# Weight loads of a decode step regrouped: wq and w1 in two loads each, w2 in one, wo in six

## The chip, the cores and the metric

The kernel runs on one core of one Trainium2 chip. The metric is the device time of one execution in microseconds (us). Kernels are compared only within the same rounds. "Faster" and "slower" mean a difference of over 2%. The profiled execution's own clock is the span, about 1.4 us shorter than the time.

TensorE does the matmuls, VectorE, ScalarE and GpSimd the rest of the arithmetic; SyncE issues the large loads, and 16 DMA engines carry them. In these profiles TensorE is granted either its full clock or half of it; the two matmuls of a row of wo follow each other every 0.215 us at the one and every 0.43 us at the other. "Half clock" below means the latter.

## The reference, cut to what matters

One token (batch 1, sequence 1, width 1024) goes through a layer norm, and then through two branches whose results are added to it:

```
xn = layernorm(x)
q  = xn @ wq                       # 1024 x 4096: 32 heads of 128
k, v = last 4096 rows of 4 key/value heads, each shared by 8 heads
attention = softmax(q k^T / sqrt(128)) v @ wo        # wo: 4096 x 1024
mlp = gelu(layernorm(xn) @ w1 + b1) @ w2 + b2        # w1: 1024 x 3584, w2: 3584 x 1024
out = x + attention + mlp
```

Each weight is used once, on one token. In bf16 that is 8.4 MB of wq, 4.2 of k, 7.3 of w1, 4.2 of v, 7.3 of w2 and 8.4 of wo: 39.85 MB to fetch, for little arithmetic.

## The kernel before

All large loads are issued on SyncE's queue in the order wq, k (2 blocks), w1, k (2 blocks), v, w2, wo. A weight is viewed as so many "rows" a partition, and a load takes a few rows, the same for all 128 partitions. The lists at the head say how many rows each load takes:

```
WQ_CHUNKS = [1, 3, 4]
W1_CHUNKS = [2, 2, 2, 2]
W2_CHUNKS = [14, 14]
WO_CHUNKS = [15, 9, 5, 2, 1]
WO_IN_W1 = sum(WO_CHUNKS[:2])
```

Each load has its own semaphore. GpSimd turns the landings of wq and w1 into row counts (L260), on which TensorE's loops wait row by row:

```
for sems, chunks, rows in ((s_wq, WQ_CHUNKS, r_wq), (s_w1, W1_CHUNKS, r_w1)):
    for j, nr in enumerate(chunks):
        pool.wait_ge(sems[j], 16)
        pool.sem_inc(rows, nr)
# ... cut ...
with nc.Fori(0, KC, 1, engines=TENSOR) as k:            # the h stage: xn @ w1
    pe.wait_ge(r_w1, k + 1)
    # ... 8 matmuls a row (L387) ...
```

TensorE's order is: q (L335), h (L387), the scores against k (L403, each block first transposed by VectorE at L344), PV (L504), w2 (L537), wo (L548) and the last row of wo (L557). w2 goes where wq was, so it is issued when q is done; 24 rows of wo go where w1 was, when h is done, and 8 rows where k was, when the scores are done. At the end TensorE takes wo's loads as they land:

```
pe.wait_ge(DVE.sem, d_op)
r = 0
for j, nj in enumerate(WO_CHUNKS[:-1]):
    pe.wait_ge(s_wo[j], 16)
    for _ in range(nj):
        for n in range(2):
            pe.matmul(ACC[n], lhsT=OP[:, r:r + 1], rhs=wo_at(r, 1)[:, n * 512:(n + 1) * 512],
                      start=False, stop=False)
        r += 1
# ... cut: the last load's row is done the same way in a block of its own (L557),
#     then the sums are copied (L567, L569) and stored ...
```

## Time and profile before

| | before |
|---|---|
| time, first 3 runs | 98.78 us median (98.74 to 98.83) |
| span of the profiled run | 97.7 us, granted TensorE clock 0.878 |
| fetched | 39.86 MB, 408 GB/s over the span |
| large loads | 22, of which 17 ahead of wo |
| TensorE matmuls busy | 68.9 us |

How to read it: a transfer that has been issued early stands in a queue, so its time to landing is mostly the time of what is ahead of it: wo's 9 rows land 42.1 us after their issue, and are 5.5 us of the stream themselves. The landing is the moment that counts, and it is the issue's start plus the time to landing. The 16 DMA engines work from about 1 us to about 95 us (SyncE's first packet of data starts at 1.01, wo's last packet ends at 94.75, and 36 of the page's 40 slices have a busy share of 90% or more), so the rest of the kernel can only add to that. The lines are shown in the prediction.

### The profile page before, as it was taken

How to read it: one execution, taken by the hardware profiler on the slowest of the kernel's cores; microseconds unless marked ns; L12 is line 12 of the kernel's file. 1: busy time of each engine (PE TensorE's matmuls, PEld its weight loads, DVE VectorE, ACT ScalarE, POOL GpSimd, SP SyncE). 2: the span in 40 equal slices, each digit the busy share in tenths (PEclk: the TensorE clock that was granted, in tenths of full speed). 3: DMA queues.
4: the chain of work that ended last, by engine and by line, in shares of the span. 5: the costliest groups of instructions: out<-in, count | busy, mean ns of one | idle time of the engine just before them, and what ended most of it. 6: DMA issues, size and time to landing. Idle time of an engine off the chain costs nothing.

```text
span 97.7 us, 1056 instructions
## 1 busy us (share of the span) xinstructions
PE 68.9 (71%) x330; PEld 32.0 (33%) x330; DVE 36.6 (37%) x49; ACT 5.8 (6%) x11; POOL 7.1 (7%) x23
## 2 busy tenths in 40 slices
PE   0002299959992999878996364279994799891991
PEld 0002255525541556435542112033341333330330
DVE  3708530000008999600999534794005300000002
ACT  0500060000001000000000000400000000000002
POOL 6795000000000000000000000000000000000000
PEclk9999999999999669999999955555699759999579
DMA  5999999999999999999999999999999999899960
GB/s 171 449 455 465 397 429 429 429 392 426 443 452 393 399 452 423 440 402 429 429 429 423 423 486 423 481 411 399 493 423 389 428 428 516 355 423 419 399 267 8
DMA packets 3205, 39.88 MB, mean 408 GB/s; under 512 B 370, under 2 KB 388, under 8 KB 644
## 3 DMA queue, kind: packets, MB, share of 16 engines
q1 hardware_dynamic: 3170, 39.85, 96.1%
q8 instruction: 1, 0.02, 0.1%
q10 hardware_dynamic: 34, 0.01, 0.1%
HBM read 39.86 MB, written 0.00 MB: 408 GB/s over the span
## 4 chain that ended last, share of the span: by engine, by line
DMA 84%; PE 9%; SPq 4%; issue 1%; DVE 1%; POOLq 0%
DMA W<-in_A_wo_dram 43%; DMA W<-in_B_w_dram 41%; PE PS L548 5%; PE PS L387 3%; SPq L178 1%; SPq L168 1%; SPq L162 1%; DVE KV L567 1%; SPq L426 0%; PE PS L557 0%; POOLq L260 0%
## 5 line engine op out<-in xcount | busy, mean ns | idle before, releaser
L344 DVE STREAM_TRANSPOSE KV<-KV 128x4096 bf16<-128x4096 bf16 x4 | 17.5, 4424 | 5.7 <-DMA KV<-in_A_k_cache_dram 5.7
L335 PE MATMUL PS<-WA,PT 128*97 x64 | 15.8, 410 | 1.4 <-POOLq L260 1.2
L387 PE MATMUL PS<-W,YZ 128*97 x64 | 14.7, 387 | 1.2 <-POOLq L260 1.2
L335 PEld LDWEIGHTS PS<-WA,PT 128*97 x64 | 8.6, 134 | 8.2 <-issue 4.1
L387 PEld LDWEIGHTS PS<-W,YZ 128*97 x64 | 8.6, 135 | 7.3 <-issue 4.6
L504 PE MATMUL PS<-KV,PT 128*32 128x512 bf16 x32 | 9.9, 484 | 0.1
L403 PE MATMUL PS<-KV,LQ 128*128 x32 | 7.8, 399 | 2.3 <-DVE KV L344 2.3
L548 PE MATMUL PS<-W,OP 128*1 128x512 bf16 x48 | 7.0, 451 | 2.2 <-DMA W<-in_A_wo_dram 2.2
L537 PE MATMUL PS<-WA,GT 128*1 128x512 bf16 x56 | 7.9, 452 | 0.0
L567 DVE CAST KV<-PS 1x512 bf16<-1x512 f32 x1 | 0.7, 683 | 18.8 <-PE PS L557 18.8
L347 DVE STREAM_TRANSPOSE TT<-PS 128x1024 f32<-128x1024 f32 x1 | 1.3, 1251 | 15.8 <-PE PS L335 15.8
L295 PE MATMUL PS<-XT,meanf 128*128 128x16 f32 x2 | 0.6, 386 | 9.1 <-DVE XT L291 9.1
L504 PEld LDWEIGHTS PS<-KV,PT 128*32 128x32 bf16 x32 | 3.7, 117 | 5.9 <-issue 4.0
L403 PEld LDWEIGHTS PS<-KV,LQ 128*128 x32 | 3.2, 99 | 6.5 <-issue 3.8
L548 PEld LDWEIGHTS PS<-W,OP 128*1 128x1 bf16 x48 | 2.2, 92 | 6.6 <-DMA W<-in_A_wo_dram 2.5
L537 PEld LDWEIGHTS PS<-WA,GT 128*1 128x1 bf16 x56 | 2.7, 96 | 4.7 <-issue 2.5
L295 PEld LDWEIGHTS PS<-XT,meanf 128*128 128x128 f32 x2 | 0.5, 312 | 9.1 <-DVE XT L291 9.1
L509 DVE TENSOR_TENSOR TT<-PS,RM 32x512 f32<-32x512 f32 x1 | 0.7, 679 | 7.1 <-PE PS L504 7.1
L451 ACT ACTIVATE Pe<-PS,NMB 128x512 bf16<-128x512 f32 x2 | 1.3, 684 | 29.0 <-DVE NMB L448 29.0
L205 DVE MEMSET PS<- 128x3072 f32 x1 | 2.6, 2618 | 0.6 <-issue 0.6
L569 ACT ACTIVATE KV<-PS 1x512 bf16<-1x512 f32 x1 | 0.6, 587 | 29.6 <-PE PS L557 29.6
L430 DVE TENSOR_REDUCE MXP<-PS 128x1 f32<-128x1024 f32 x1 | 1.2, 1225 | 2.7 <-PE PS L403 2.7
(87 smaller groups left out, 33.0 us busy)
## 6 DMA issues: line engine op xcount, KB each, us to landing
W<-in_B_w_dram SPq DMA_DIRECT2D x4, 1792.0 KB, 34.1
WA<-in_B_w_dram SPq DMA_DIRECT2D x2, 3584.0 KB, 40.5
WA<-in_A_wq_dram SPq DMA_DIRECT2D x1, 4096.0 KB, 20.7
KV<-in_A_k_cache_dram SPq DMA_DIRECT2D x4, 1024.0 KB, 33.1
KV<-in_A_v_cache_dram SPq DMA_DIRECT2D x4, 1024.0 KB, 33.9
W<-in_A_wo_dram SPq DMA_DIRECT2D x1, 3840.0 KB, 37.0
WA<-in_A_wq_dram SPq DMA_DIRECT2D x1, 3072.0 KB, 11.4
W<-in_A_wo_dram SPq DMA_DIRECT2D x1, 2304.0 KB, 42.1
```

Of the source, the lines that this page charges most:

```text
L205: d_ps = DVE.mark(dve.memset(PS[:, 0:6 * 512], 0.0))
L335: last = pe.matmul(PS[0:97, n * 512:(n + 1) * 512], lhsT=shifted(XZ, s)[:, bass.ds(k, 1), :], rhs=wq_rows[:, bass.ds(k, 1), s * 1024 + n * ...
L344: dve.transpose(out=KT[:, g * W:(g + 1) * W], in_=KT[:, g * W:(g + 1) * W]).then_inc(r_k, 1)
L347: DVE.mark(dve.transpose(out=TT[:, :], in_=PS[:, 0:1024]))
L387: last = pe.matmul(PS[0:97, (2 + n) * 512:(2 + n) * 512 + HW], lhsT=shifted(YZ, s)[:, bass.ds(k, 1), :], rhs=w1_rows[:, bass.ds(k, 1), c: ...
L403: last = pe.matmul(PS[:, (4 + n) * 512:(5 + n) * 512], lhsT=q_blocks[:, bass.ds(g, 1), j, :], rhs=k_blocks[:, bass.ds(g, 1), n, :, j, :], ...
L430: d_mxp = DVE.mark(dve.tensor_reduce(out=MXP[:, 0:1], in_=PS[:, 4 * 512:6 * 512], axis=AX.X, op=ALU.max))
L451: a_exp = ACT.mark(act.activation(out=Pe[:, n * 512:(n + 1) * 512], in_=PS[:, (4 + n) * 512:(5 + n) * 512], func=ACTF.Exp, scale=SCALE, bi ...
L504: last = pe.matmul(PS[0:32, 0:512].rearrange("p (g d) -> p g d", g=HKV), lhsT=PT[:, b * 32:(b + 1) * 32], rhs=Vb[:, b, :, :], start=(b == ...
L537: pe.matmul(ACC[n], lhsT=GT[:, c:c + 1], rhs=W2[:, c * D + n * 512: c * D + (n + 1) * 512], start=False, stop=False)
L548: pe.matmul(ACC[n], lhsT=OP[:, r:r + 1], rhs=wo_at(r, 1)[:, n * 512:(n + 1) * 512], start=False, stop=False)
L567: d_out = DVE.mark(dve.tensor_copy(OUT[32:33, :], ACC[1]))
```

## The change

The intent is fewer and larger loads ahead of wo, and finer ones at the end, so that the transfers finish a little sooner and little work follows the last landing. The diff in full:

```
-WQ_CHUNKS = [1, 3, 4]
-W1_CHUNKS = [2, 2, 2, 2]
-W2_CHUNKS = [14, 14]
-WO_CHUNKS = [15, 9, 5, 2, 1]
+WQ_CHUNKS = [4, 4]
+W1_CHUNKS = [4, 4]
+W2_CHUNKS = [28]
+WO_CHUNKS = [15, 9, 4, 2, 1, 1]
```

## The prediction

> **What bounds the kernel now.** I read the page's slices first, then the chain of waits, then the timeline around each load that is regrouped. In the slices (granted TensorE clock, DMA busy share, GB/s, in 40 slices of 2.44 us) the reader is to see that the 16 DMA engines have no hole:
>
> ```profile
> PEclk9999999999999669999999955555699759999579
> DMA  5999999999999999999999999999999999899960
> GB/s 171 449 455 465 397 429 429 429 392 426 443 452 393 399 452 423 440 402 429 429 429 423 423 486 423 481 411 399 493 423 389 428 428 516 355 423 419 399 267 8
> ```
>
> 39.85 MB at some 427 GB/s are 93.3 us, of a span of 97.7. The chain (start us, us, what) says the same: two loads stand for 84% of it, and TensorE comes in at the end alone.
>
> ```profile
> 4.22 39.67 DMA W<-in_B_w_dram
> ...
> 44.20 1.69 PE PS L387 x8
> ...
> 45.92 1.73 PE PS L387 x8
> ...
> 48.04 42.10 DMA W<-in_A_wo_dram
> ...
> 90.18 5.30 PE PS L548 x32
> 95.48 0.23 PE PS L557 x2
> ...
> 95.74 0.68 DVE KV L567
> ```
>
> The 42.10 us are no cost of that load; it stood in the queue behind k, v and w2. What the chain calls a path through L387 is slack: wo is issued at 47.67, and w2 lands only at 75.6 (issue at 32.4 plus the longest time to landing of its line, 43.2), so a later issue of wo starves nobody for 27 us.
>
> The tail is nearly a tie of two things. Issue plus landing gives wo's loads: 15 rows at 84.7, 9 rows at 90.14, 5 rows at 57.79 + 35.4 = 93.2, 2 rows at about 94.5, the last row at about 58.65 + 36.4 = 95.05. Against these the timeline (start us, us, engine, line, what, count, idle before it) has:
>
> ```profile
> 84.78 3.40 PE L548 MATMUL PS<-W,OP 128*1 128x512 bf16 x30 [0.24 <-DMA W<-in_A_wo_dram]
> 90.18 3.57 PE L548 MATMUL PS<-W,OP 128*1 128x512 bf16 x18 [2.00 <-DMA W<-in_A_wo_dram]
> 93.54 1.95 PE L548 MATMUL PS<-KV,OP 128*1 128x512 bf16 x14
> 95.32 0.38 PE L557 MATMUL PS<-KV,OP 128*1 128x512 bf16 x2
> ```
>
> TensorE waits 2.0 us for the 9-row load, then never again: 18 rows from 90.18 to 95.7, some rows at half clock (a pair, one row, takes 0.43 us at half clock and 0.215 us at full; the table by stretches gives a clock of 0.58 from 90.2 to 93.2). The last row starts at 95.32, only about 0.25 us after it landed. So TensorE's backlog sets the end, and the transfer stands 0.2 us behind it as a floor.
>
> [...]9 and 15 rows of wo took 5.46 and 9.06 us. [...]the 6 rows between those two sizes (1.573 MB in 3.60 us) mean 437 GB/s; 9 rows at that rate are 5.40 us, leaving 0.06 for the load itself, and 5 rows (1.311 MB) are 3.00 of the 3.05 us, leaving 0.05. [...]half clock in slices 13 to 14, and for some 3.4 us after 90.66.
>
> **The change part by part.**
>
> *w1 in 4+4.* Rows 0 to 3 now start when the second quarter has landed, at 35.4 rather than 31.0, and rows 4 to 7 at 43.9, when all has. Before:
>
> ```profile
> 31.70 7.94 PE L387 MATMUL PS<-W,YZ 128*97 x32
> ...
> 39.96 3.40 PE L387 MATMUL PS<-W,YZ 128*97 x16 [0.33 <-POOLq L260]
> ...
> 44.20 3.43 PE L387 MATMUL PS<-W,YZ 128*97 x16 [0.84 <-POOLq L260]
> ...
> 46.37 8.77 DVE L344 STREAM_TRANSPOSE KV<-KV 128x4096 bf16<-128x4096 bf16 x2 [5.68 <-DMA KV<-in_A_k_cache_dram]
> ...
> 47.63 5.35 PE L403 MATMUL PS<-KV,LQ 128*128 x24
> ...
> 55.31 2.44 PE L403 MATMUL PS<-KV,LQ 128*128 x8 [2.33 <-DVE KV L344]
> ```
>
> After: rows 0 to 3 take 6.8 us at full clock (2 x 3.4) and some 8.6 with a cold start, so 35.5 to 44.1; rows 4 to 7 follow, 6.8 us, to 50.9. That is 3.3 us later than 47.63. The scores of three k blocks then take 5.2 us at full clock, to 56.1, and the fourth, whose transpose ends at 55.14, 1.75 us to 57.8. Before they ended at 57.75. The wait of 2.33 us for VectorE, and the half clock that followed it, swallow the delay. **Net at the end of the scores: 0, give or take 0.5 us.** Everything behind them (softmax, PV, w2, wo) keeps its place.
>
> *wq in 4+4.* The q matmuls start at 12.2 today, held by the layernorm of x, and four rows have landed at 12.05 in either form: nothing lost. But x's packets now pass between packets of 32 KB rather than 24 KB a partition row: estimated from bytes, a turn goes from 0.9 to 1.2 us, and with 3 or 4 turns x lands 1 to 2 us later. q then starts at about 13.5 and, partly catching up its 1.25 us wait at 22.2, ends at 29.5 to 30.5 rather than 29.3. The h matmuls start at 35.5: hidden.
>
> *w2 in one load.* TensorE must wait for all 28 rows; they land at 75.6, or a little sooner, and it reaches them at 76.64, after PV:
>
> ```profile
> 76.64 7.89 PE L537 MATMUL PS<-WA,GT 128*1 128x512 bf16 x56
> ```
>
> Cost 0, with 1.0 us to spare. I expect w2 at 76.6 and the first 15 rows of wo at about 84.7, as now.
>
> *wo 15 9 4 2 1 1.* Rows 24 to 27 land at some 92.5 rather than 93.2, but TensorE only reaches them at 93.54: worth nothing while it is behind. One more load and wait: about 0.06 us of transfer.
>
> *Number of loads.* 22 large loads become 19. Ahead of the 9 rows of wo there are four fewer (wq one, w1 two, w2 one): 4 x 0.05 = 0.2 us earlier. At the end three fewer, 0.15 us.
>
> **The sum.** The 9 rows land at 89.95; the same backlog of 18 rows then ends 0.2 us sooner; the floor of the last row falls by 0.15 us and stays behind it. 98.78 - 0.2 = 98.58; I say **98.6 us**.
>
> **Rivals.** (a) *The later h stage goes through to the end.* If the clock stays half for 3.4 us longer, scores end at about 59.4, w2 at 86.2, the 15 rows at 89.6: still before 90. TensorE has 2.0 us of slack there, so the end moves only for a delay above that; twice the delay would cost 1.5 us: 100.3. Against: rows 0 to 3 lie in 8.5 us of waiting time. (b) [...]the 18 rows take 3.9 us instead of 5.5 and the last row's landing is the bound: 95.05 - 0.15 + one row; that gives about 98.4, no better. (c) *The big loads stream worse*, with 57 KB a row or late x: for it nothing in the trace, since 28 and 30 KB rows are the fastest there; 1% of rate would be 0.9 us: 99.5. [...]
>
> **Range and chances.** Nothing here takes bytes away, so 2% (96.8) is out of reach; a gain is at most some 0.4 us, to 98.3. A loss needs a delay above 2 us in a chain with slack. Range 98.25 to 99.15. Faster 0.01, same 0.97, slower 0.02.
>
> **What would show it.** Right: bytes and DMA share unchanged; h from about 35.5 to 51, scores ended at 57.3 to 58.3; x seen by VectorE at 8.4 to 9.4; w2's first matmul at 76 to 77; wo's 9 rows landed at 89.9 to 90.0, and TensorE with no long wait behind them. Wrong: a hole in the DMA row, scores that end after 59.5, w2's matmuls waiting for a DMA, or a last wait of TensorE for wo's last row, which would make the transfer the bound and not the backlog.

Passages that say more than the traces show are cut out of the recorded text, and the cuts are marked. Its sum came to 98.78 - 4 x 0.05 = 98.58. The 0.05 us for a load is an estimate from the 5.46, 9.06 and 3.05 us that loads of wo took in the kernel before. Rival (b): full clock to the end, 18 rows at 0.215 us; what would bring it was not shown. Rival (d), that the loads' own cost is hidden (98.8), named a mechanism that no trace shows.

The estimates that give no source can be had from the profile of the kernel before. The "cold start" is one at half clock: the first four rows of h took 7.94 us there, with half clock from 32.63 to 36.05, and the next two pairs of rows 3.40 and 3.43; 6.8 us and half of 3.41 are 8.5. For x: its four packets of 512 bytes start at 5.76 to 6.09, among packets of wq that take 0.91 us with 24 KB and 1.21 with 32 KB. The first 4-byte packet of their queue starts 0.93 us after the first of them, and in the changed kernel 1.23 us (6.68 after 5.45): a turn of 0.9 and of 1.2 us. VectorE gets x at 7.38. For rival (c): packets of 28, 30 and 32 KB all moved 27.0 GB/s an engine, those of 8 KB 26.5.

## The result, and the profile after

The changed kernel takes 98.83 us (median of 4 runs, 98.74 to 99.01), the kernel before beside it 98.81 (4 runs, 98.74 to 98.96). The ratio is 1.0002 with a 95% interval of 0.9983 to 1.0021: the same. A ratio here and below is the mean time of one kernel's fast runs over that of the other's in the same rounds, so it is not quite the ratio of the medians.

The slices of the changed kernel (clock, DMA busy share, GB/s):

```profile
PEclk9999999999999655999999999955699759999579
DMA  7999999989999989979999998889994999899970
GB/s 215 430 432 431 431 430 430 430 346 426 490 446 470 399 376 517 423 336 430 430 430 423 423 671 376 376 376 399 634 470 201 428 466 466 383 408 401 413 272 8
```

The 4 in the DMA row looks like a hole and is none. The rates about it are 634, 470 and then 201 GB/s, and 634 (like 671 before it) is more than the 516 at which the kernel before has its highest slice; w2's packets are now rows of 57 KB that take 2.1 us, and such a packet is evidently counted in one slice. The packet records show no idle engine there, and w2 lands at 29.29 + 46.2 = 75.49, against 75.6 before.

The chain of waits of the changed kernel (start us, us, what):

```profile
2.69 41.17 DMA W<-in_B_w_dram
...
44.17 1.69 PE PS L387 x8
...
51.43 38.63 DMA W<-in_A_wo_dram
...
90.10 5.30 PE PS L548 x32
95.41 0.24 PE PS L557 x2
```

It has the old form: wo is issued 3.4 us later, waits 3.5 us less in the queue, and lands 0.08 us sooner, at 90.06. The timeline of TensorE's matmuls shows what became of the later h stage:

```profile
35.71 7.93 PE L387 MATMUL PS<-W,YZ 128*97 x32 [3.97 <-POOLq L260]
...
44.17 6.86 PE L387 MATMUL PS<-W,YZ 128*97 x32 [0.53 <-POOLq L260]
...
51.03 7.08 PE L403 MATMUL PS<-KV,LQ 128*128 x32
...
64.47 9.73 PE L504 MATMUL PS<-KV,PT 128*32 128x512 bf16 x32
...
76.53 7.89 PE L537 MATMUL PS<-WA,GT 128*1 128x512 bf16 x56
```

h ends at 51.03 instead of 47.63. The scores, which used to stop for 2.33 us for the last transposed block, now run through and end at 58.11 instead of 57.75. PV starts 0.05 us later than before (64.42), w2 0.11 us sooner (76.64). The delay of 3.4 us is gone by then. The end of the same timeline:

```profile
84.70 3.40 PE L548 MATMUL PS<-W,OP 128*1 128x512 bf16 x30 [0.28 <-DMA W<-in_A_wo_dram]
...
90.10 3.78 PE L548 MATMUL PS<-W,OP 128*1 128x512 bf16 x18 [2.00 <-DMA W<-in_A_wo_dram]
...
93.66 1.74 PE L548 MATMUL PS<-KV,OP 128*1 128x512 bf16 x14
...
95.24 0.38 PE L557 MATMUL PS<-KV,OP 128*1 128x512 bf16 x2
```

The last matmuls start 0.08 us sooner than before, as much as the 9 rows landed sooner. The weight load of that last row now waits 0.15 us for its transfer, which it did not before: in small, the last of the prediction's own signs of being wrong.

So three things had to be explained. Why did four loads fewer ahead of wo bring 0.08 us and not 0.2? Why does even that not show in the time? And how much delay can the stages ahead of wo bear? My theory was that of the prediction, with a price for each load; the rivals were that a large first load is slow to start, that the price is hidden, that the delay does go through, and that the clock sets the end.

### The profile page after: what moved, and what is told of

It is laid out like the page before. It is cut to its first block, busy times and chain, and to the rows that moved or that the text cites. A ratio compares the mean times of both kernels' runs of the same rounds, so it can differ in the third digit from the quotient of the medians.

```text
span 97.6 us, 1050 instructions
## 1 busy us (share of the span) xinstructions
PE 67.3 (69%) x330; PEld 31.8 (33%) x330; DVE 36.0 (37%) x49; ACT 5.8 (6%) x11; POOL 7.1 (7%) x23
## 4 chain that ended last, share of the span: by engine, by line
DMA 82%; PE 13%; SPq 2%; issue 1%; DVE 1%; POOLq 0%
DMA W<-in_B_w_dram 42%; DMA W<-in_A_wo_dram 40%; PE PS L387 7%; PE PS L548 5%; SPq L168 1%; DVE KV L567 1%; SPq L178 0%; SPq L426 0%; SPq L162 0%; PE PS L557 0%; POOLq L260 0%
## 5 line engine op out<-in xcount | busy, mean ns | idle before, releaser
L548 PE MATMUL PS<-W,OP 128*1 128x512 bf16 x48 | 7.2, 461 | 2.3 <-DMA W<-in_A_wo_dram 2.3
L403 PE MATMUL PS<-KV,LQ 128*128 x32 | 7.1, 379 | 0.0
L548 PEld LDWEIGHTS PS<-W,OP 128*1 128x1 bf16 x48 | 2.2, 94 | 6.8 <-DMA W<-in_A_wo_dram 2.5
## 6 DMA issues: line engine op xcount, KB each, us to landing
WA<-in_B_w_dram SPq DMA_DIRECT2D x1, 7168.0 KB, 46.2
```

The source lines that it names most:

```text
L403: last = pe.matmul(PS[:, (4 + n) * 512:(5 + n) * 512], lhsT=q_blocks[:, bass.ds(g, 1), j, :], rhs=k_blocks[:, bass.ds(g, 1), n, :, j, :], ...
```

## The experiments

Each edit is to the kernel before unless it says otherwise, and all results are correct. The intervals of experiments 3, 7, 10 and 11 lie wholly above 1. Each run was profiled once.

"Landing" is issue plus time to landing. The profile gives the latter to 0.1 us, and a landing waits for the slowest of the 16 DMA engines: for wo's 9 rows in the kernel before, the engines' last writes end at 89.16 to 89.80, and the chain has the landing at 90.14. Where hundredths matter there is a steadier measure: the packet records hold 16 small semaphore writes for each load, and the mean of their times is called "the stream" below.

**1. wq alone in 4 and 4.**

```
-WQ_CHUNKS = [1, 3, 4]
+WQ_CHUNKS = [4, 4]
```

> Kernel before with wq alone in two loads of four rows. My theory (a load costs its own 0.05 to 0.06 us of stream time, nothing else): k's first block lands 0.05 us earlier than 24.25, and the time falls by 0.05 us. Rival (a 4-row load is slow to start, as the 33 ns longer packets at the head of the changed kernel's trace hint): x is seen by VectorE at about 8.3 rather than 7.4, the first k block lands at 24.28 or later, no gain. In both the time stays within 0.2 us of before: q ends at about 29.3, because its second half waits for the second load.

98.97 us against 98.98 (ratio 1.0000, 0.9973 to 1.0028). The first k block lands at 1.18 + 23.3 = 24.48, later than the 24.25 before, and VectorE sees x at 8.29. By the stream, wq is through at 21.31, before at 21.13. The rival was right about the head: one load fewer, and a loss there. More was to be learned from the end of this run's timeline, TensorE's matmuls again:

```profile
90.12 2.11 PE L548 MATMUL PS<-W,OP 128*1 128x512 bf16 x18 [1.96 <-DMA W<-in_A_wo_dram]
93.20 1.84 PE L548 MATMUL PS<-KV,OP 128*1 128x512 bf16 x14 [0.97 <-DMA KV<-in_A_wo_dram]
95.06 0.38 PE L557 MATMUL PS<-KV,OP 128*1 128x512 bf16 x2
```

The loads of wo are those of the kernel before and land at the same times to 0.06 us. Yet the 18 matmuls take 2.11 us instead of 3.57, TensorE then waits 0.97 us, and the last row starts at 95.06 and not at 95.32. In this execution the clock was full to the end. The half clock comes in stretches of 3.41 us or a multiple (3.41, 6.83 and 13.65 in the two profiles compared), and where they fall differs from run to run: in the profile before one lay from 90.66 to 94.07, in the one after from 90.38 to 93.79, here none did.

**2. w1 alone in 4 and 4.**

```
-W1_CHUNKS = [2, 2, 2, 2]
+W1_CHUNKS = [4, 4]
```

> Kernel before with w1 alone in two loads of four rows. My theory (the later h stage is swallowed by the wait for the fourth k transpose): h ends at about 51.0 instead of 47.6, scores end at 57.6 to 58.2 instead of 57.8, PV and w2 begin where they did (64.4 and 76.6, each within 0.3 us), the last w1 load lands 0.1 to 0.16 us earlier, time within 0.2 us of before. Rival (the delay passes to the end): w2 begins at 78 or later, 9 rows of wo wait less than 1 us, time 1 us or more above before.

98.89 us against 98.98 (ratio 0.999, 0.9962 to 1.0018). h ends at 50.99, the scores at 58.07, PV starts at 64.44, and w2 at 75.38: the rival, a delay that goes through, is out. w2 is even sooner than expected, because half clock ended at 67.61 in this run and at 70.18 in the profile before, so that PV took 8.62 us and not 9.89. The landing of the last w1 load, 3.2 + 40.7 = 43.9, is too coarse a figure for two loads fewer; by the stream w1 ends at 43.21, before at 43.31.

**3. w2 in 14 loads of two rows.**

```
-W2_CHUNKS = [14, 14]
+W2_CHUNKS = [2] * 14
```

> Kernel before with w2 in 14 loads of two rows instead of 2 of fourteen, the same bytes. My theory (each further load costs stream time: [...]0.06 us): 12 loads more put the landing of all of w2 and of wo 0.6 to 0.85 us later, and the time rises by the same, to 99.4 to 99.65. Rival (the cost of a load is hidden behind the queue): landings and time within 0.15 us of before.

99.46 us (99.31 to 99.51) against 98.98; ratio 1.0042 (1.0015 to 1.007). TensorE gets the 9 rows of wo at 90.73 instead of 90.18, and the last row at 95.67:

```profile
90.73 2.11 PE L548 MATMUL PS<-W,OP 128*1 128x512 bf16 x18 [0.27 <-DMA W<-in_A_wo_dram]
```

So 12 loads more cost 0.55 us, 0.046 us each; by the stream, w2 takes 17.48 us instead of 16.95, which is 0.044 for each. The price of a load is real, somewhat below the 0.05 to 0.07 that I had put in. Each load here is 128 packets, so what a load costs and what 8 packets an engine cost are not separated.

**4. The changed kernel with wq in 1, 3 and 4 again.**

```
-WQ_CHUNKS = [4, 4]
+WQ_CHUNKS = [1, 3, 4]
```

> The changed kernel with wq again in loads of 1, 3 and 4 rows. If the first 4-row load is what ate the gain: the first k block lands at 24.24, the 9 rows of wo at about 89.95 (changed kernel 90.06, before 90.14), and the time is 0.1 us below the changed kernel's. If loads count alone: 0.05 us later than the changed kernel.

99.01 us against 98.98 (ratio 0.9999, 0.997 to 1.0029). The first k block lands at 24.2 as expected, but the 9 rows of wo at 90.13, 0.07 us later than in the changed kernel, about what "loads count alone" expects. By the stream the second k block is through 0.12 us sooner than in the changed kernel (26.08, there 26.20), and the first load of w1 0.12 us later (34.91, there 34.79): what the head won was lost again in that stretch, and more.

**5. wq in 1 and 7.**

```
-WQ_CHUNKS = [1, 3, 4]
+WQ_CHUNKS = [1, 7]
```

> Kernel before with wq in two loads of 1 and 7 rows: the same number of loads as the change's 4 and 4, but a small first load. If a large first load is slow to start (wq in 4 and 4 put the first k block at 24.28 and 24.48, three loads with a small first at 24.2 to 24.25): the first k block lands at 24.15 to 24.22. If two loads of wq are at fault: 24.3 or later. q waits for 7 rows at 21.9 and ends at about 34 rather than 29.3, still ahead of the h matmuls' last rows; time within 0.2 us of before.

98.83 us against 98.77 (ratio 0.9999, 0.998 to 1.0018). The first k block lands at 1.18 + 23.2 = 24.38, which by my expectation speaks against "a large first load is slow to start". But over all runs, those with three loads of wq have this landing at 24.05 to 24.25, those with two at 24.18 to 24.48: the ranges overlap, and experiment 9, with the same loads of wq, has 24.28. The stream separates them. wq is through at 21.07 to 21.19 with loads of 1, 3 and 4 (nine profiles), at 21.17 and 21.22 with 1 and 7 (experiments 9 and 5), and at 21.26 to 21.31 with 4 and 4 (three profiles). The packets say where: those that start before 4.2 us take longer than packets of their size do later, in sum 0.33 to 0.50 us an engine where the first load has one row, and 0.58 to 0.67 us where it has four. So the large first load is slow to start, and a small one mends the greater part; why it is slow is not shown.

q ends at 36.5 here, where 34 was expected, and w2 starts 1.0 us later than before; the end did not move.

**6. w1 in 2 and 6, a larger delay.**

```
-W1_CHUNKS = [2, 2, 2, 2]
+W1_CHUNKS = [2, 6]
```

> Kernel before with w1 in loads of 2 and 6 rows: a larger delay of h than the change's. Six rows start at 44.0 and take 10.3 us at full clock and up to 13 from a cold start: h ends at 55.8 to 57.2, scores at 63 to 64.5, 5 to 6 us later than before. My theory (the chain has 2 to 4 us of slack ahead of the last rows of wo, and no more): w2 begins at 81 to 83, the end moves by 1 to 3 us, time 100 to 102, wo's matmuls no longer wait for a load. Rival (the transfers hide any such delay): within 0.3 us of before.

The 13 us "from a cold start" are an estimate: 10.3 us in the prediction's ratio of 8.6 to 6.8.

98.79 us (98.68 to 98.87) against 98.77; ratio 0.9991 (0.9973 to 1.001). My expectation of 100 to 102 was wrong. TensorE's matmuls:

```profile
55.71 7.07 PE L403 MATMUL PS<-KV,LQ 128*128 x32
...
80.56 6.21 PE L537 MATMUL PS<-WA,GT 128*1 128x512 bf16 x56
86.60 5.52 PE L548 MATMUL PS<-W,OP 128*1 128x512 bf16 x48
93.05 1.84 PE L548 MATMUL PS<-KV,OP 128*1 128x512 bf16 x14 [0.92 <-DMA KV<-in_A_wo_dram]
94.92 0.38 PE L557 MATMUL PS<-KV,OP 128*1 128x512 bf16 x2
```

The scores end 5.0 us later than before, w2 starts 3.9 us later, w2 ends 2.2 us later (it took 6.21 us and not 7.89), and then 24 rows of wo run without a stop, so that TensorE is waiting again before the 5-row load. I had taken the half-clock durations of the profile as fixed, and in this run w2 and wo ran at full clock. That they did so because the work was pushed together is not shown: w2 took 6.21 us in experiments 2, 3, 5 and 8 too. So of the delay of 5.0 us at the scores 2.2 us were left at the end of w2, hardly more than the 2.0 us of idle time that I had read off.

**7. wo's 9-row load split.** Here the border between the two places for wo moves with the list, so that the same 24 rows stay in w1's place.

```
-WO_CHUNKS = [15, 9, 5, 2, 1]
-WO_IN_W1 = sum(WO_CHUNKS[:2])
+WO_CHUNKS = [15, 5, 4, 5, 2, 1]
+WO_IN_W1 = sum(WO_CHUNKS[:3])
```

> Kernel before with wo in 15, 5, 4, 5, 2 and 1 rows: the 9-row load is split, so that rows 15 to 19 can be used at about 87.8. My theory (in runs at half clock at the end, the backlog of the 9-row load sets it; at full clock the landing of the last row does): the last row's matmul starts within 0.1 us of its landing in either phase of the clock, TensorE waits for a load before it, the span is 97.3 to 97.5 in all runs, where before has 97.4 to 97.7; the median falls by 0.0 to 0.2 us. Rival (the backlog doesn't matter): no difference in any run, or 0.05 us more for one more load.

99.90 us (98.80 to 100.06, six runs) against 98.77; ratio 1.0069 (1.0027 to 1.0112). Four runs lie at 99.9 to 100.1, two at 98.80 and 99.03. It is the opposite of my expectation. One of the four slower runs was profiled; the end of its timeline:

```profile
90.13 1.03 PE L548 MATMUL PS<-W,OP 128*1 128x512 bf16 x8 [0.99 <-DMA W<-in_A_wo_dram]
93.17 3.02 PE L548 MATMUL PS<-KV,OP 128*1 128x512 bf16 x14 [2.01 <-DMA KV<-in_A_wo_dram]
95.98 0.64 PE L557 MATMUL PS<-KV,OP 128*1 128x512 bf16 x2
```

There is no backlog at 93.13, when the 5 rows land. But TensorE had been idle for 0.99 and 2.01 us, and half clock is granted from 93.34 to 96.75: the last seven rows take 3.02 us. The last row starts at 95.98; in experiment 9, whose last packet ends at the same time (94.70, here 94.68), it starts at 95.03. In the kernel before the half clock came earlier, from 90.66, while there were still loads to wait for.

**8. wo alone in 15, 9, 4, 2, 1 and 1.**

```
-WO_CHUNKS = [15, 9, 5, 2, 1]
+WO_CHUNKS = [15, 9, 4, 2, 1, 1]
```

> Kernel before with wo alone in 15, 9, 4, 2, 1 and 1 rows. My theory (one more load 0.05 us, its wait already met or hidden): the last row lands at 95.05 to 95.15, time within 0.15 us of before, in both phases of the clock.

99.06 us against 99.05 (ratio 1.0006, 0.9987 to 1.0026). In its profile, at full clock, TensorE waits for each of wo's loads, and starts the last row at 95.11, as the last load lands. The finer end is neither gain nor loss.

**9. A version for speed.** wq in 1 and 7, w1 in 4 and 4, w2 in one, wo as in experiment 7.

```
+WQ_CHUNKS = [1, 7]
+W1_CHUNKS = [4, 4]
+W2_CHUNKS = [28]
+WO_CHUNKS = [15, 5, 4, 5, 2, 1]
+WO_IN_W1 = sum(WO_CHUNKS[:3])
```

> A version for speed: wq in 1 and 7 rows, w1 in 4 and 4, w2 in one load, wo in 15, 5, 4, 5, 2 and 1. Sum of what the runs point to: small first load (0.2 us less than the changed kernel at the head), four loads fewer ahead of wo (0.2 us less), no backlog at the end: all of wo lands at 94.8 to 94.95 rather than 95.05, time 0.2 to 0.3 us below before. Rival (another stretch takes back what fewer loads give, as the stretch from 27 to 33 us seems to do): landing at 95.0 to 95.1, time within 0.1 us of before.

98.85 us (98.79 to 99.51) against 98.77; ratio 1.0013 (0.9986 to 1.004). It beats neither kernel, and the rival was right: the last row is had at 95.03, not at 94.8 to 94.95. Its end, though, has the loads of experiment 7 and lets one see the clock alone:

```profile
86.02 5.35 PE L548 MATMUL PS<-W,OP 128*1 128x512 bf16 x48
93.17 1.84 PE L548 MATMUL PS<-KV,OP 128*1 128x512 bf16 x14 [1.80 <-DMA KV<-in_A_wo_dram]
95.03 0.38 PE L557 MATMUL PS<-KV,OP 128*1 128x512 bf16 x2
```

From the same start, 93.17, the same 14 matmuls take 1.84 us at full clock here and 3.02 us there. Here w2 came later and the 24 rows ran together, and there was no half clock after 81.8.

**10. and 11. Eight matmuls more in the idle time before wo's 9 rows**, in the kernel before and in the changed one:

```
 for j, nj in enumerate(WO_CHUNKS[:-1]):
+    if j == 1:
+        for _ in range(8):
+            pe.matmul(PS[0:1, 0:512], lhsT=OP[:, 0:1], rhs=wo_at(0, 1)[:, 0:512], start=True, stop=True)
     pe.wait_ge(s_wo[j], 16)
```

> Kernel before with eight more matmuls on TensorE ahead of the wait for wo's 9 rows (into a bank that nobody reads; the result stays right), about 1.7 us of the 2.0 us in which it idled. Theory (the half clock after 90.66 comes from that idle time and is what puts TensorE's backlog behind the last landing): full clock from 84 to the end, TensorE waits for the 5-row load and for the last row, the last matmul starts at 95.0 to 95.1 rather than 95.32, all spans 97.3 to 97.5, median 0 to 0.2 us below before. Rival (the half clock has another cause, or the backlog is set by the load itself): half clock after 90.3 to 91 as before and the last matmul at 95.2 or later.

> The changed kernel with the same eight matmuls. Theory: as in the kernel before, full clock at the end, the last matmul starts at 95.0 to 95.1 within 0.1 us of the last row's landing, spans 97.3 to 97.5; the changed kernel and the kernel before are then equal within 0.1 us, because both end with the same bytes. Rival (fewer loads pay once the clock is out of the way): 0.1 to 0.2 us below the filled kernel before.

100.24 us (99.89 to 101.01) and 100.53 us (99.91 to 101.03) against 99.05; ratios 1.0143 (1.0107 to 1.018) and 1.0161 (1.0123 to 1.0199). The runs don't test what they were made for, and that the half clock comes from the idle time stays an assumption. In the filled kernel before, w2 still lands at 32.3 + 43.2 = 75.5, but TensorE gets wo's 15 rows only at 86.12 rather than at 84.78 (L551 is L548 of the kernel before):

```profile
86.12 4.73 PE L551 MATMUL PS<-W,OP 128*1 128x512 bf16 x30 [3.00 <-DMA W<-in_A_wo_dram]
```

One line of its DMA queues differs (the page's part on queues: packets, MB, share):

```profile
q8 instruction: 2, 0.03, 0.1%
```

The kernel before has one such packet, at 96.12, after its last matmul. Here, with 1,072 instructions on the page instead of 1,056, there are two, and the packet records show the further one at 79.58 (at 79.33 in the filled changed kernel): 16,384 bytes in 0.93 us, and a data packet right after it that took 1.64 us instead of 1.14. Together that is 1.4 us, about what wo's landing lost. It is one engine's loss: by the mean over the engines the 15 rows are through at 84.13, before at 84.06, but the last of the 16 writes comes 1.85 us after the first and not 0.64. That the longer program brought the further packet is my reading of these two runs.

**12. All of w1 in one load.**

```
-W1_CHUNKS = [2, 2, 2, 2]
+W1_CHUNKS = [8]
```

> Kernel before with all of w1 in one load, the largest delay of h. Loads of 2 and 6 rows were absorbed in whole: w2 ran in 6.2 us at full clock instead of 7.9, and 24 rows of wo ran without a wait. With that counted in: h starts at 44.0 and ends at 59 to 60.5, scores at 66 to 68, w2 starts at 84 to 86 and takes 6.2 us, 24 rows of wo 5.2 us and 8 rows 1.7 us, so the last matmul starts 1.5 to 3 us later than before: time 100.3 to 101.9. Rival (nothing ahead of the transfers matters): within 0.3 us of before.

Three runs took 101.91 to 102.14 us, all counted as slow (over 1.5% above the fastest run of the kernel), and one fast run 99.06, against 99.05 before. The profile is of a slow run, so I draw nothing from it; how much delay beyond experiment 6 can be borne stays open.

## Why the prediction was right or wrong

98.6 us was predicted, in a range of 98.25 to 99.15, with 97% for "the same". Measured is 98.83, the same within 0.2%. That was safe: with the bytes unchanged, nothing in the prediction's own list of outcomes reaches 2%. The gain of 0.2 us that was forecast did not come; its ratio, 0.998, lies just outside the measured interval. By its steps:

**The bound is the stream of transfers: right.** The same bytes land at the same time to 0.1 us, and TensorE's stages ahead of them may move without the end moving (experiments 2 and 6).

**w1: right, and for the reason given.** h from 35.7 to 51.0, scores to 58.1, no wait for the fourth transpose, and everything behind in its place. Experiment 2 shows it for w1 alone. But rival (a), "twice the delay would cost 1.5 us: 100.3", was wrong: experiment 6 delays the scores by 5.0 us and takes 98.79. The sum took the durations of one profile as fixed, and w2 alone took 6.21 or 7.89 us, by the clock of the run.

**wq: right that x comes later and that it costs nothing; its size smaller.** x reaches VectorE at 8.27, 0.9 us later, where 1 to 2 us were estimated. That the size of the passing packets does it (0.91 us for 24 KB, 1.21 for 32 KB) agrees with the other runs: 7.1 to 7.5 with loads of 1, 3 and 4, 8.3 with 4 and 4, 9.0 with 1 and 7. q starts at 12.52, only 0.3 us later and not at 13.5: the cast that follows on VectorE (L289) took 0.77 us before, and ended as GpSimd's last fill (L254) did, at 8.8; in the changed kernel it took 0.17 us. q ends at 29.26 as before, since its own wait of 1.2 us at 22.2 took the rest. What was missed is the slow start of the large load (next step but one).

**w2: right.** It lands at 75.49 and is first used at 76.53.

**The number of loads: the term that was mis-sized.** "4 x 0.05 = 0.2 us earlier" became 0.08. What the runs have for wo's 9 rows, the landing (from the chain, or 0.04 us ahead of TensorE's start, or issue plus time to landing) and the stream, against the number of loads ahead of wo:

| run | loads ahead of wo | 9 rows land, us | stream, us |
|---|---|---|---|
| before | 17 | 90.14 | 89.52 |
| 8 (wo in six) | 17 | 90.09 | 89.57 |
| changed | 13 | 90.06 | 89.44 |
| 4 (changed, wq 1, 3, 4) | 14 | 90.13 | 89.56 |
| 2 (w1 4 and 4) | 15 | 90.08 | 89.43 |
| 6 (w1 2 and 6) | 15 | 89.97 | 89.35 |
| 1 (wq 4 and 4) | 16 | 90.08 | 89.48 |
| 5 (wq 1 and 7) | 16 | 90.10 | 89.49 |
| 3 (w2 in 14) | 29 | 90.69 | 90.12 |

Between 13 and 17 loads the landings lie within 0.17 us and in no order, and the two kernels with the same loads up to there differ by 0.05. The stream, taken in stretches, says why:

- After w1 it is regular. Loads of wo with 1, 2, 4, 5, 9 and 15 rows take 0.646, 1.248, 2.453, 3.055, 5.465 and 9.079 us, which is 0.602 for a row (435 GB/s) and 0.044 for the load. w2 takes 16.91 us in one load (four profiles), 16.95 to 16.97 in two (eight, the slow run of experiment 12 left out) and 17.48 in fourteen. So the one load of w2 that went away did bring its price, 0.04 us.
- At the head it went the other way. The second k block is through at 26.20 instead of 26.04, although wq has one load fewer: the slow start of the large first load (experiment 5) cost more than the load that it saved.
- From there to the fourth row of w1 the stream takes 8.53 to 8.79 us in the seven profiles with two loads of w1 there, 8.75 in the kernel before and 8.59 in the changed one. This is 0.16 us in the change's favour, and more than one load; what makes this stretch vary stays open.
- The second half of w1 takes 8.48 us instead of 8.52, the price of one load.

In sum 0.16 lost, 0.16 won, and twice 0.04 won: 0.08 us. So the price of a load was nearly right (0.044, not 0.05 to 0.06), and the step that failed is that it was to be won wherever a load goes away. That even the 0.08 doesn't show in the time is no wonder, with 0.2 us and more between runs.

**The end: right for some runs only.** "TensorE's backlog sets the end, and the transfer stands 0.2 us behind it as a floor" holds where half clock falls on the last rows, as in the two profiles compared and in experiment 4. Where it doesn't (experiments 1, 2, 5, 6, 8 and 9), TensorE waits for the last rows and the floor is the end, at 94.9 to 95.1. The loads of wo of both kernels were seen with both cases (experiments 1 and 8 have them at full clock), and the difference, 0.26 us for the kernel before, is larger than the 0.08 us won. This accounts for a part of the spread between runs, though not shown for all of it. That the two profiles compared fell in the same case is luck.

Which case it is was a near thing. In these traces the clock changes only at the ends of stretches of 3.41 us. In the stretch that ends about when the 9 rows arrive, TensorE's matmuls took 1.41 us in the kernel before (87.25 to 90.66), 1.41 in the changed one (86.97 to 90.38), and 1.39 in experiment 4, and half clock followed; they took 1.45 us in experiment 1 (86.71 to 90.12) and 1.48 in experiment 5, and full clock stayed. In experiment 7 it was the stretch after that (89.93 to 93.34), with 1.20 us of matmuls, that half clock followed. In all 14 profiles, as far as the clock is on record, full clock was lost after no such stretch with over 1.67 us of matmuls and kept after none with under 1.45. So 0.04 us of matmuls in that stretch (1.41 against 1.45) lay between the two ends, and the stretches begin at different times from run to run. That this decides the end is my reading of these profiles. The finer split of wo is worth nothing in either case, as predicted, and the floor was rightly said to leave little to win.

**Readings and sums of the prediction that are wrong.** Behind the wait for the 9 rows come 17 rows (9, 5, 2 and 1), not 18. Four rows of wq land at 0.80 + 11.4 = 12.2, not 12.05, hardly before q starts at 12.23; in experiment 1 q waits 0.50 us for them. The 15 rows took 9.08 us by the stream, not 9.06; with that the rate is 435 GB/s and not 437, and the rest for a load is 0.044 us. Half clock came to slices 13 to 14, from 32.63, although TensorE's matmuls took 1.67 us of the 3.41 us before it. Two signs of being right were just missed: x at 8.27 (8.4 to 9.4), the 9 rows at 90.06 (89.9 to 90.0).

## What to carry to other kernels

When the transfers run without a hole, count bytes first: grouping the same bytes into fewer loads was worth hundredths of a microsecond each (0.044 us here), a large load at the very head cost more than that (about 0.2 us here: wq was through at 21.26 to 21.31 with 4 and 4, at 21.07 to 21.19 with 1, 3 and 4), and a delay ahead of the last loads was free where TensorE caught up in time (5.0 us at the scores in experiment 6, at a ratio of 0.9991). Judge the end by what TensorE has to do after the last landings and at which clock: in experiment 7 half clock fell on the last rows after waits of 0.99 and 2.01 us, and 14 matmuls took 3.02 us, though after the same loads they took 1.84 us at full clock in experiment 9. Don't take a difference of 0.1 us from one profile of each kernel; look first at how far profiles with the same loads lie apart (0.05 us for wo's 9 rows in the two kernels with the same loads up to there). Before you trust an experiment that adds instructions, look whether the page's line of the instruction queue changed too: in experiment 10 one packet more there went with a loss of 1.3 us at TensorE's next load.
